# A causal convolution ahead of two matmul layers: units cut into overlapping blocks, five on TensorE and four off it

## The chip, the cores and the metric

The kernel runs on one core of a Trainium2 chip. A core has five engines that this text calls TensorE (PE in the profile, its weight loads PEld), VectorE (DVE), ScalarE (ACT), GpSimd (POOL) and SyncE (SP), which here issues nearly all transfers. The metric is the device time of one execution in microseconds (us); lower is better. Three runs of the kernel before gave 710.38, 710.92 and 711.0, a median of 710.92.

## The reference

`x` is 8 sequences of 4096 tokens with 192 channels in float32. There are 8 heads of 24 neighbouring channels; each has 7 taps, the softmax of a row of `weight`. The convolution looks back over 7 tokens, and every sequence begins with zeros:

```python
w = softmax(weight)                                   # 8 heads x 7 taps
x_pad = concatenate([zeros((B, 6, D)), x], axis=1)
out[b, s, h, g] = sum(w[h, k] * x_pad[b, s + k, h, g] for k in range(7))
```

The result, 32768 tokens by 192 channels, goes through two layers with a gate between them:

```python
h = x @ w_in            # 192 -> 2048
g = h * np.cos(h)
out = g @ w_out         # 2048 -> 192
```

## The kernel before, in words

**Tiles and units.** A tile `t` is 512 tokens, and there are 64. A unit `u` is 1024 tokens, two tiles: the even tile of the unit and the odd one. Four units make a sequence. Convolution, casts, loads and transposes go by units and are done some units ahead; the two layers go by tiles.

**The two layers.** `mm1(t, j)` makes 256 of the 2048 hidden columns of a tile, for j = 0 to 7; the text calls these eight h0 to h7. It takes three channel groups of 64, and each of them on the upper and the lower 64 rows of the array at once, so one h is six matmuls of 64 rows by 512 tokens (L475). The result fills one of three `h` buffers in PSUM, of two banks each. `gcu` puts the cosine on ScalarE (L483) and the product with h on VectorE (L487); the product frees the buffer. `mm2_step` (L525) adds pairs of such matmuls of 192 columns into the output banks `o_ps`, 64 steps a tile, while the next tile's h are made. Half-way through a tile's steps the two row halves change banks; a `Turn` (L176) makes TensorE's first matmul after the change wait for an empty instruction on the SP queue, which itself waits for the matmuls before the change. A tile's output is copied from PSUM by ScalarE and VectorE (`evac`, L544) and stored from SP (L547).

**The convolution before, from unit 4 on.** A unit has eight blocks of 128 tokens. Six of them (`NPE = UB - 2`) are convolved on TensorE: token rows times a band matrix per head, which holds the taps on its diagonals (`conv_mm`, L222). One `conv_part` does four heads, and a tile has one of them: 8 matmuls of 64 rows by 144 columns, 4 and 4 around a `Turn`, into an `h` buffer. ScalarE copies it out (`conv_out`, L237, two copies of 288 elements), GpSimd writes every 64 channels twice (`double_unit`, L290) so that both row halves get them, and one transposing transfer on SP (`turn_unit`, L303, 18 squares of 128 by 128) puts channels on partitions in `cT`.

The other two blocks are cast, transposed as they are (`turn_raw`, L321, with the edges 6 squares) and convolved with channels on partitions: ScalarE multiplies with three of the taps (`taps_act`, L327), GpSimd with four and adds (`conv_raw`, L336 to L342), and two transfers carry each result to the other row half (`spread_raw`, L349).

A block convolved by itself lacks the six tokens before it, so the first six tokens of every block are wrong. `load_edges` (L77) loads 16 tokens around each block's start, and `mend_edges` (L365 to L371) makes the six tokens again on GpSimd. Units 1 to 3 have smaller variants of this; unit 0 is done apart, at the start.

**What sets the order.** There is no scheduler: each engine runs its instructions in the order in which the code records them, and two strings of marks give this order for every tile. In the first, hj is an h, mN are N steps of the second layer, q the half-way change, c1 and c2 the halves of a `conv_part`, and K, T, L, X, Y, D, R, U, O cast, raw transpose, load, transpose, mend, double, raw convolution, spread and store. In the second, sj is cosine and product, aj.. a tap, e.. a conv copy, P and Q the two evacuations. P and the taps are ScalarE's, Q is VectorE's:

```python
PE_ORDER = "m11 h0 m4 h1 U m6 h2 m7 q Y R K h3 m7 h4 m7 c1 m4 c2 X T L m5 h5 m9 p h6 D O h7 m4"
ACT_ORDER = "s0 a00 s1 s2 a12 s3 s4 ec1 ec2 Q s5 P s6 s7 a27"
```

K, R and X are done in the even tile of a unit, and D, L, Y, T, U and the three taps in the odd one.

Of the kernel before, what the change touches and what calls it, by code (L numbers as in the profile page):

```python
# [16 lines left out]
def kernel(  # L17
# [8 lines left out]
    nc = tc.nc  # L26
# [18 lines left out]
    FIRST_RAW = 2 * 2  # L45
    NPE = UB - 2
    W = 128 - (K - 1)
    PA = 3

# [7 lines left out]
    raw_pool = ctx.enter_context(tc.tile_pool(name="raw", bufs=2))  # L57
# [77 lines left out]
    xb0 = xbf_pool.tile([128, UB + 1, D], BF16, name="x_bf")  # L135
# [17 lines left out]
    wn = consts.tile([128, HQ, K], BF16)  # L153

# [30 lines left out]
    bf = {}  # L185

    def cast_unit(u, n0=0, n1=UB + 1, copy=nc.gpsimd.tensor_copy):
        if n0 == 0:
            bf[u] = xb0 if u == 0 else xbf_pool.tile([128, UB + 1, D], BF16, name="x_bf")
        if u >= FIRST_RAW:  # L190
            raw[u] = raw_pool.tile([128, 2, NC, 2, 64], BF16, name="raw")

            def part(out, m0, m1):
                copy(out=out, in_=x_tiles[u][:, m0:m1, :].rearrange("p n (h r k) -> p (n h) k r", k=NC, r=R))  # L194


            for t in range(2):
                copy(out=raw[u][:, 0, :, t, :].rearrange("p k (h r) -> p h k r", r=R),  # L198
                     in_=x_tiles[u][:, NPE + t, :].rearrange("p (h r k) -> p h k r", k=NC, r=R))
            for t in range(2):  # L200
                copy(out=raw[u][:, 1, :, t, :].rearrange("p k (h r) -> p h k r", r=R),
                     in_=x_tiles[u][:, UB, :].rearrange("p (h r k) -> p h k r", k=NC, r=R))
            if u % UPS == 0:
                nc.gpsimd.memset(raw[u][0:8, 1], 0.0)
            part(bf[u][:, 0:NPE, :].rearrange("p n (h k r) -> p (n h) k r", k=NC, r=R), 0, NPE)
            bf.pop(u - 2, None)
            return
# [4 lines left out]
        if u and u % UPS == 0:  # L212
            nc.gpsimd.memset(bf[u][0:8, UB, :], 0.0)
        bf.pop(u - 2, None)
# [4 lines left out]
    def conv_mm(u, c, ps, i, rows, n0, n1, prev=0, **flags):  # L219

        h = 4 * c + i
        return nc.tensor.matmul(  # L222
            out=ps[i // 2][:, 0 : (n1 - n0) * 2 * G].rearrange("p (n k i r) -> p i n k r", n=n1 - n0, k=NC, i=2)[:, i % 2],
            lhsT=band[rows, h, 128 if prev else 0 : 256 if prev else 128],
            rhs=bf[u][rows, n0:n1, h * G : (h + 1) * G].rearrange("p n (k r) -> p n k r", k=NC),
            skip_group_check=True, **flags)

    def conv_out(u, c, ps, n0, m0, m1, copy, double=False, banks=(0, 1)):

        for b in banks:  # L230
            w0 = (2 * c + b) * 2 * R
            o = ct_tiles[u][:, m0:m1, :, :, w0 : w0 + 2 * R].rearrange("p n k t w -> p (n k) t w")
            i = ps[b][:, (m0 - n0) * 2 * G : (m1 - n0) * 2 * G].rearrange("p (m t w) -> p m t w", t=1, w=2 * R)
            if double:
                copy(o, i.to_broadcast([128, (m1 - m0) * NC, 2, 2 * R]))
            else:
                copy(o[:, :, 0, :], i[:, :, 0, :])  # L237
# [8 lines left out]
    def conv_part(u, c, banks, whole=False):  # L246
# [3 lines left out]
        nb = NPE if u >= FIRST_RAW else UB + (u == 1)  # L250
        sides = [slice(0, 64), slice(64, 128)]

        def mm(i, rows, **flags):
            return conv_mm(u, c, ps, i, sides[rows], 0, nb, **{"start": False, "stop": False, **flags})

        if whole:
            for i in range(4):
                conv_mm(u, c, ps, i, slice(0, 128), 0, nb, start=i % 2 == 0, stop=i % 2 == 1)
            if u == 2 and c == 0:
                spread_taps(ps[1][:, UB * 2 * G : UB * 2 * G + K])  # L260
            yield
        else:
            mm(0, 0, start=True)
            mm(2, 1, start=True)
            turn = Turn()
            turn.mark(mm(1, 0), mm(3, 1))
            yield
            turn.wait(mm(2, 0), mm(0, 1))
            mm(3, 0, stop=True)
            mm(1, 1, stop=True)  # L270
# [3 lines left out]
        for b in range(2):  # L274
            conv_out(u, c, ps, 0, 0, nb, nc.scalar.copy, banks=(b,))
            if b and u == 2 and c == 0:
                nc.scalar.copy(tap, ps[1][:, UB * 2 * G : UB * 2 * G + K])
            if b:
                have.add(("conv", u, c))
            yield  # L280
# [3 lines left out]
    def double_unit(u):  # L284
# [4 lines left out]
        nb = NPE if u >= FIRST_RAW else UB + (u == 1)  # L289
        nc.gpsimd.tensor_copy(out=ct[:, 0:nb, :, 1, :], in_=ct[:, 0:nb, :, 0, :])  # L290
        for t in range(2) if 1 < u < FIRST_RAW else ():
            nc.gpsimd.tensor_copy(out=ct[:, UB, :, t, :].rearrange("p k (h r) -> p k h r", r=R),
                                  in_=bf[u][:, UB, :].rearrange("p (h k r) -> p k h r", k=NC, r=R))

    def turn_unit(u, n0=0, n1=UB + 1):
        assert ("double", u) in have
        have.update((("turn", u), ("whole", u, 1)) if u == 0 else (("turn", u),))
        ct = ct_tiles.pop(u)
        if u >= FIRST_RAW:
            n1 = NPE  # L300
        if u not in cT:
            cT[u] = cT_pool.tile([128, UB + 1, NC, 128], BF16, name="cT")
        nc.sync.dma_start_transpose(out=cT[u][:, n0:n1].rearrange("p n c k -> p (n c) k"),  # L303
# [13 lines left out]
    raw, rT, pa = {}, {}, {}  # L317

    def turn_raw(u):
        rT[u] = rT_pool.tile([128, 2, NC, 128], BF16, name="rT")  # L320
        nc.sync.dma_start_transpose(out=rT[u].rearrange("p n c k -> p (n c) k"),  # L321
                                    in_=raw.pop(u).rearrange("p n c t k -> p (n c t k)"))

    def taps_act(u, j):
        if j == 0:
            pa[u] = pa_pool.tile([128, PA, NC, W], FP32, name="pa")
        nc.scalar.mul(pa[u][:, j], rT[u][:, 0, :, j : j + W], tap[:, j : j + 1])  # L327

    raw_prod = consts.tile([128, K - PA, NC, W], FP32)

    def conv_raw(u):

        cT[u] = cT_pool.tile([128, UB + 1, NC, 128], BF16, name="cT")
        a, p = pa.pop(u), raw_prod
        for j in range(PA, K):
            nc.gpsimd.tensor_scalar(out=p[:, j - PA], in0=rT[u][:, 0, :, j : j + W], scalar1=tap[:, j : j + 1], scalar2=None,  # L336
                                    op0=ALU.mult)
        nc.gpsimd.tensor_tensor(out=p[:, 0:PA], in0=p[:, 0:PA], in1=a, op=ALU.add)  # L338
        nc.gpsimd.tensor_tensor(out=p[:, 0:2], in0=p[:, 0:2], in1=p[:, 2:4], op=ALU.add)  # L339
        for t in range(2):  # L340
            rows = slice(64 * t, 64 * t + 64)
            nc.gpsimd.tensor_tensor(out=cT[u][rows, NPE + t, :, K - 1 : 128], in0=p[rows, 0], in1=p[rows, 1], op=ALU.add)  # L342

    def spread_raw(u):

        have.add(("raw", u))
        for t in range(2):
            of, to = slice(64 * t, 64 * t + 64), slice(64 - 64 * t, 128 - 64 * t)
            nc.sync.dma_start(out=cT[u][to, NPE + t, :, K - 1 : 128], in_=cT[u][of, NPE + t, :, K - 1 : 128])  # L349

    edge_prod = consts.tile([128, NC * UB, K - 1, K], FP32)

    def mend_edges(u):
# [3 lines left out]
        if u == 1:  # L357
            nc.gpsimd.tensor_copy(out=cT[u][:, 0:UB, :, 0 : K - 1],
                                  in_=cT[u][:, UB].rearrange("p c (n t) -> p n c t", t=16)[:, :, :, 8 : 8 + K - 1])
            return  # L360
        edges = rT.pop(u)[:, 1] if u >= FIRST_RAW else cT[u][:, UB]
        edges = edges.rearrange("p c (n t) -> p (c n) t", t=16)
        window = edges[:, :, 2 : 2 + K]
        window = bass.AP(window.tensor, window.offset, [*window.ap[:2], [1, K - 1], [1, K]])
        nc.gpsimd.tensor_tensor(out=edge_prod, in0=window,  # L365
                                in1=tap.rearrange("p (a b k) -> p a b k", a=1, b=1).to_broadcast([128, NC * UB, K - 1, K]),
                                op=ALU.mult)
        nc.gpsimd.tensor_tensor(out=edge_prod[:, :, :, 0:3], in0=edge_prod[:, :, :, 0:3], in1=edge_prod[:, :, :, 3:6], op=ALU.add)  # L368
        for j in (1, 2):
            nc.gpsimd.tensor_tensor(out=edge_prod[:, :, :, 0], in0=edge_prod[:, :, :, 0], in1=edge_prod[:, :, :, j], op=ALU.add)  # L370
        nc.gpsimd.tensor_tensor(out=cT[u][:, 0:UB, :, 0 : K - 1].rearrange("p n c t -> p c n t"),  # L371
# [322 lines left out]
```

## Time and profile before

| what | value |
|---|---|
| median of 3 runs | 710.92 us |
| the profiled execution, and its span | 710.74 us, 709.0 us |
| TensorE busy | 702.8 us, 99% |
| VectorE busy | 640.2 us, 90% |
| ScalarE busy | 621.0 us, 88% |
| GpSimd busy | 598.6 us, 84% |
| granted TensorE clock | 1.00 over the span |
| transfers' queue q1 | 50.3% of 16 engines' span |

Busy is the union of an engine's instructions; overlapping ones count once. A matmul's recorded end is modelled, so what TensorE really spends is read from start to start: a pair of matmuls on the two row halves starts some 216 ns after the last pair at 512 columns. Issuing a transfer isn't counted as busy, but it holds the queue that issues it for the time that its line shows. In a timeline's line the columns are start and length in us, engine, line of the code, operation, output<-input, shapes, and count; the bracket gives the idle time before it and who ended it.

The page's costliest groups of GpSimd, by line, mean length of one: L336 products 1209 ns (366 elements), L338 sums 2518 (1098), L339 sums 1738 (732), L342 sums 829 (366 on half the partitions), L365 edge products 2237 (1008), L368 1013 and L370 556 edge sums, L290 doubling 1144 (1152), L194 casts 1758 (1152). In two units, 299 to 342 us, these and the smaller ones keep GpSimd busy 40.4 of 43 us.

### The profile page before, as it was taken

What the parts mean: (1) busy time and instruction counts of PE and PEld (TensorE: products, weight loads), DVE (VectorE), ACT (ScalarE), POOL (GpSimd) and SP (SyncE); (2) the same over time, 40 slices, a digit from 0 to 9 for tenths busy, and PEclk for the clock granted to TensorE, in tenths of its full rate; (3) what the DMA queues carried; (4) which work ended last, traced back from release to release, by engine and by line L of the source; (5) the groups of instructions that cost most, each with busy time, mean ns of one, the idle gap of its engine ahead of it and who ended that gap; (6) DMA issues with size and microseconds to landing.
All of it is one profiled execution on the core that took longest, in us unless ns stands there. A gap on an engine that the chain in (4) does not pass through costs nothing.

```text
span 709.0 us, 27153 instructions
## 1 busy us (share of the span) xinstructions
PE 702.8 (99%) x11836; PEld 532.8 (75%) x11838; DVE 640.2 (90%) x598; ACT 621.0 (88%) x803; POOL 598.6 (84%) x588
## 2 busy tenths in 40 slices
PE   8999999999999999999999999999999999999997
PEld 4677777777777777777777777777777777777776
DVE  6889998999999999999999999999999999999996
ACT  7888989898989898998889898989898989988875
POOL 6554999999999999999999999999999999997900
PEclk9999999999999999999999999999999999999999
DMA  8974546446446455364465364564553553643311
GB/s 210 241 153 103 117 115 144 83 129 148 103 128 139 83 134 145 97 138 85 126 145 120 112 147 83 126 147 107 124 131 90 136 134 103 142 93 67 85 46 46
DMA packets 185510, 85.17 MB, mean 120 GB/s; under 512 B 113456, under 2 KB 185008, under 8 KB 185392
## 3 DMA queue, kind: packets, MB, share of 16 engines
q1 hardware_dynamic: 184680, 82.47, 50.3%
q8 instruction: 92, 1.51, 0.9%
q0 software_dynamic: 416, 0.79, 0.7%
q14 instruction: 26, 0.21, 0.1%
q10 hardware_dynamic: 296, 0.20, 0.1%
HBM read 31.36 MB, written 25.17 MB: 80 GB/s over the span
## 4 chain that ended last, share of the span: by engine, by line
PE 96%; DMA 1%; DVE 1%; POOL 0%; SPq 0%; ACT 0%; issue 0%; POOLq 0%
PE o_ps L525 47%; PE h L475 47%; PE h L222 2%; DMA wo_f<-in_moe_w_out_dram 1%; PE h L525 0%; SPq L105 0%; DVE band L393 0%; POOL wo L101 0%; POOL mask L140 0%; DVE ct L416 0%; PE o_ps L410 0%; ACT mask L145 0%; DVE diag L382 0%; DVE prod L379 0%; DVE o_sb L554 0%
## 5 line engine op out<-in xcount | busy, mean ns | idle before, releaser
L487 DVE TENSOR_TENSOR g<-h,cs 128x1024 bf16<-128x1024 f32 (+1 forms) x513 | 602.7, 1216 | 25.3 <-ACT cs L483 22.5
L483 ACT ACTIVATE cs<-h 128x1024 bf16<-128x1024 f32 (+1 forms) x513 | 509.4, 1023 | 69.2 <-PE h L475 54.9
L525 PEld LDWEIGHTS <-g 64*128 64x128 bf16 x8192 | 366.1, 94 | 92.0 <-issue 0.7
L525 PE MATMUL o_ps<-wo,g 64*128 64x192 bf16 x8128 | 430.4, 243 | 0.2 <-POOL wo L101 0.2
L475 PE MATMUL h<-cT,w 64*128 64x512 bf16 (+1 forms) x3078 | 411.7, 376 | 0.7 <-DVE g L487 0.4
L475 PEld LDWEIGHTS <-w 64*128 64x128 bf16 x3078 | 160.1, 94 | 71.1 <-issue 1.8
L336 POOL TENSOR_SCALAR raw_prod<-rT,tap 128x366 f32<-128x366 bf16 x112 | 133.6, 1209 | 0.0
L338 POOL TENSOR_TENSOR raw_prod<-raw_prod,pa 128x1098 f32<-128x1098 f32 x28 | 70.5, 2518 | 0.0
L544 DVE COPY o_sb<-o_ps 128x384 f32<-128x384 f32 x62 | 34.6, 557 | 34.1 <-PE o_ps L525 33.9
L365 POOL TENSOR_TENSOR edge_prod<-rT,tap 128x1008 f32<-128x1008 bf16 x28 | 62.6, 2237 | 0.2
L290 POOL COPY ct<-ct 128x1152 bf16<-128x1152 bf16 (+2 forms) x31 | 36.6, 1181 | 28.8 <-ACT ct L237 27.5
L237 ACT CAST ct<-h 128x288 bf16<-128x288 f32 (+2 forms) x124 | 44.8, 412 | 8.3 <-PE h L222 5.0
L339 POOL TENSOR_TENSOR raw_prod<-raw_prod 128x732 f32<-128x732 f32 x28 | 48.7, 1738 | 2.2
L327 ACT ACTIVATE pa<-rT,tap 128x366 f32<-128x366 bf16 x84 | 50.5, 601 | 0.0
L342 POOL TENSOR_TENSOR cT<-raw_prod 64x366 bf16<-64x366 f32 x56 | 46.4, 829 | 4.3
L194 POOL CAST x_bf<-x_f 128x1152 bf16<-128x1152 f32 x28 | 49.2, 1758 | 0.0
L222 PE MATMUL h<-x_bf,band 64*128 64x144 bf16 (+3 forms) x480 | 37.5, 224 | 0.0
L370 POOL TENSOR_TENSOR edge_prod<-edge_prod 128x144 f32<-128x144 f32 x60 | 33.4, 556 | 4.7
L368 POOL TENSOR_TENSOR edge_prod<-edge_prod 128x432 f32<-128x432 f32 x30 | 30.4, 1013 | 2.3
L544 ACT COPY o_sb<-o_ps 128x384 f32<-128x384 f32 x64 | 30.2, 473 | 0.1
L198 POOL CAST raw<-x_f 128x192 bf16<-128x192 f32 x56 | 23.4, 446 | 1.7
L222 PEld LDWEIGHTS <-band 64*128 64x128 bf16 (+1 forms) x480 | 22.7, 94 | 1.4 <-issue 1.1
(70 smaller groups left out, 109.3 us busy)
## 6 DMA issues: line engine op xcount, KB each, us to landing
out_dram<-o_sb SPq DMA_DIRECT2D x63, 384.0 KB, 3.0
x_f<-in_x_dram SPq DMA_DIRECT2D x30, 768.0 KB, 7.3
x_f<-in_x_dram SPq DMA_DIRECT2D x31, 96.0 KB
cT<-cT SPq DMA_DIRECT2D x56, 45.8 KB, 3.0
x_f<-in_x_dram SPq DMA_DIRECT2D x4, 384.0 KB, 5.7
wo_f<-in_moe_w_out_dram SPq DMA_DIRECT2D x4, 384.0 KB, 7.0
w<-in_moe_w_in_dram POOLq DMA_DIRECT2D x2, 384.0 KB, 6.2
cT<-ct SPq DMA_TRANSPOSE x32, 4.9
```

Source lines behind the costliest of these rows:

```text
L194: copy(out=out, in_=x_tiles[u][:, m0:m1, :].rearrange("p n (h r k) -> p (n h) k r", k=NC, r=R))
L222: return nc.tensor.matmul(out=ps[i // 2][:, 0 : (n1 - n0) * 2 * G].rearrange("p (n k i r) -> p i n k r", n=n1 - n0, k=NC, i=2)[:, i % 2], ...
L327: nc.scalar.mul(pa[u][:, j], rT[u][:, 0, :, j : j + W], tap[:, j : j + 1])
L336: nc.gpsimd.tensor_scalar(out=p[:, j - PA], in0=rT[u][:, 0, :, j : j + W], scalar1=tap[:, j : j + 1], scalar2=None, op0=ALU.mult)
L338: nc.gpsimd.tensor_tensor(out=p[:, 0:PA], in0=p[:, 0:PA], in1=a, op=ALU.add)
L339: nc.gpsimd.tensor_tensor(out=p[:, 0:2], in0=p[:, 0:2], in1=p[:, 2:4], op=ALU.add)
L365: nc.gpsimd.tensor_tensor(out=edge_prod, in0=window, in1=tap.rearrange("p (a b k) -> p a b k", a=1, b=1).to_broadcast([128, NC * UB, K - 1 ...
L475: nc.tensor.matmul(out=h[:, i, n0 * 128 : n1 * 128], lhsT=w[rows, k, j, :], rhs=c[rows, m0 + n0 : m0 + n1, k, :], start=(k == 0), stop=(k ...
L483: nc.scalar.activation(out=cs[:, :, part], in_=h[:, :, part], func=AF.Sin, bias=math.pi / 2.0, scale=1.0)
L487: nc.vector.tensor_tensor(out=g_tiles[t][:, 2 * j : 2 * j + 2, part], in0=h[:, :, part], in1=cs[:, :, part], op=ALU.mult)
L525: ms.append(nc.tensor.matmul(out=o_ps[tt, b, si], lhsT=g_tiles[tt][rows, f, s * 128 : (s + 1) * 128], rhs=wo[rows, f // 2, f % 2, :], star ...
L544: (copy or copies[b])(o_sb[t][:, 2 * b : 2 * b + 2, :].rearrange("p s d -> p (s d)"), o_ps.pop((t, b)))
```

## The change

**Blocks that overlap.** From unit 4 on a unit has nine blocks of 128 tokens that overlap (`load_unit`): five that each give 112 new tokens (`NPB, OP = 5, 112`), 560 together, and four that each give 116 (`NRB`, `OR`), 464 together. A block contains the tokens before its new ones, so there are no edges: `load_edges` and `mend_edges` are gone from unit 4 on, and units 1 to 3 have their edges from the band matrix, and only copied.

**On TensorE.** `conv_unit` takes the five blocks for all eight heads at once, once a unit, in the odd tile: 16 matmuls of 64 rows by 120 columns (15 pieces of 8 elements), 8 and 8 around one `Turn`. The weights are the last 112 columns of the band. Two copies of 480 elements go into `ct_bufs`, whose squares are 64 channels wide with an empty one at each group's ends. `turn_unit` then transposes without doubling: for each of three channel groups once from the first square and once from the second, so that the row halves hold the same tokens 112 columns apart. That makes six transfers of three squares of 112 by 128, in place of one of 18. `mm1` reads the two row halves at places that differ by `OP`.

**Off TensorE.** The four other blocks are cast into the same buffer `xk`, transposed (6 squares), and convolved with channels on partitions: three taps on ScalarE as six instructions of 348 elements, four taps on GpSimd as one instruction of 2784, then three sums of 2088, 1392 and 696 elements. `spread_raw` has four transfers for two.

**Order.** The two tiles of a unit now have their own strings. `R+1` means the raw convolution of unit u + 1, and `a211` tap 2, half 1, after h1.

```diff
-    NPE = UB - 2
-    W = 128 - (K - 1)
+    NPB, OP = 5, 112
+    NRB = 4
+    OR = (U - NPB * OP) // NRB
+    WN = NC * NRB // 2
     PA = 3
+    HALF = WN // 2
+    CW = U + OP
...
     def load_unit(u, n0=0, n1=UB, queue=nc.sync):
+        if u >= FIRST_RAW:
+            x_tiles[u] = xin.tile([128, UB + 1, D], FP32, name="x_f")
+            raw = NPB * OP + OR - 128
+            for n0, n1, t0, step in ((NPB, NPB + 2, raw, 2 * OR), (NPB + 2, UB + 1, raw + OR, 2 * OR), (0, NPB, OP - 128, OP)):
+                rows = xf[u * U + t0 : u * U + t0 + 128, :]
+                rows = bass.AP(rows.tensor, rows.offset, [[D, 128], [step * D, n1 - n0], [1, D]])
+                queue.dma_start(out=x_tiles[u][:, n0:n1, :], in_=rows)
+            return
...
     def cast_unit(u, n0=0, n1=UB + 1, copy=nc.gpsimd.tensor_copy):
+        if u >= FIRST_RAW:
+            xk[u] = xk_pool.tile([128, NC * (UB + 1), 64], BF16, name="xk")
+            for n0, n1 in ((NPB, UB + 1), (0, NPB)):
+                copy(out=xk[u][:, NC * n0 : NC * n1].rearrange("p (k n) m -> p k n m", k=NC),
+                     in_=x_tiles[u][:, n0:n1].rearrange("p n (m k) -> p k n m", k=NC))
...
+    def conv_unit(u, banks):
+        ps = banks()
+        sides = [slice(0, 64), slice(64, 128)]
+        def mm(h, side):
+            first, last = h % 4 == 0 and h // 4 == side, h % 4 == 3 and h // 4 != side
+            return nc.tensor.matmul(
+                out=ps[h // 4][0:OP, 0 : NPB * 4 * G].rearrange("p (m i r) -> p i m r", m=NC * NPB, i=4)[:, h % 4],
+                lhsT=band[sides[side], h, 128 - OP : 128], rhs=xk[u][sides[side], 0 : NC * NPB, R * h : R * (h + 1)],
+                start=first, stop=last, skip_group_check=True)
+        for h in range(4):
+            ms = mm(h, 0), mm(h + 4, 1)
+        turn = Turn()
+        turn.mark(*ms)
+        yield
+        for h in range(4):
+            ms = mm(h + 4, 0), mm(h, 1)
+            if h == 0:
+                turn.wait(*ms)
+        yield
+        for b in range(2):
+            w0 = 4 * R * b
+            nc.scalar.copy(ct_bufs[u % 2][0:OP, 0 : NC * (NPB + 1)].rearrange("p (k n) m -> p k n m", k=NC)[:, :, 1:, w0 : w0 + 4 * R],
+                           ps[b][0:OP, 0 : NPB * 4 * G].rearrange("p (k n w) -> p k n w", k=NC, w=4 * R))
...
     def turn_unit(u, n0=0, n1=UB + 1):
+        if u >= FIRST_RAW:
+            cT[u] = cT_pool.tile([128, NC * (UB + 1) * 128], BF16, name="cT")
+            for k in range(NC):
+                to = cT[u][:, k * CW : k * CW + (NPB + 1) * OP].rearrange("p (n s t) -> p s n t", s=2, t=OP)
+                for s in range(2):
+                    m = (NPB + 1) * k + s
+                    nc.sync.dma_start_transpose(out=to[:, s], in_=ct_bufs[u % 2][0:OP, m : m + NPB + 1].rearrange("p s m -> p (s m)"))
...
-    def taps_act(u, j):
+    def taps(u, j, half, mul):
+        part = slice(HALF * half, HALF * (half + 1))
+        mul(pa[u][:, j, part], tap_window(u, j)[:, part], tap[:, j : j + 1])
...
     def conv_raw(u):
+        nc.gpsimd.tensor_tensor(out=p, in0=tap_window(u, PA, K),
+                                in1=tap[:, PA:K].rearrange("p (j a b) -> p j a b", a=1, b=1).to_broadcast([128, K - PA, WN, OR]),
+                                op=ALU.mult)
...
     def spread_raw(u):
+        for to, t0 in ((0, NPB * OP + OP), (1, NPB * OP)):
+            rows = slice(64 * to, 64 * to + 64)
+            d = c[rows, :, t0 : t0 + NRB * OR].rearrange("p k (v t) -> p k v t", v=2)
+            for v in range(2):
+                nc.sync.dma_start(out=d[:, :, v], in_=r[64 * v : 64 * v + 64])
...
     def mm1(t, j, n0=0, n1=NB):
+                if t >= TPU * FIRST_RAW:
+                    t0 = k * CW + (t % TPU) * T + n0 * 128 + (0 if i else OP)
+                    rhs = c[rows, t0 : t0 + (n1 - n0) * 128]
...
-    PE_ORDER = "m11 h0 m4 h1 U m6 h2 m7 q Y R K h3 m7 h4 m7 c1 m4 c2 X T L m5 h5 m9 p h6 D O h7 m4"
-    ACT_ORDER = "s0 a00 s1 s2 a12 s3 s4 ec1 ec2 Q s5 P s6 s7 a27"
+    PE_ORDER = ['m12 h0 m4 h1 m5 R+1 h2 K+3 m7 q h3 m6 h4 m17 h5 U+0 X+1 m9 p h6 h7 O m4', 'm11 h0 m4 h1 m6 h2 m7 q h3 m5 h4 T+3 m7 c1 m8 c2 L+4 m3 h5 m9 O h6 p h7 m4']
+    ACT_ORDER = ['s0 s1 a211 s2 s3 s4 a014 a114 Q s5 P s6 s7 a007', 's0 s1 s2 a102 s3 a203 s4 Q ec2 ec1 s5 P s6 s7']
```

More of the change, by code (lines that the diff above doesn't have):

```diff
@@ L132 @@
     keep_warm(9)
-    xb0 = xbf_pool.tile([128, UB + 1, D], BF16, name="x_bf")
+    xb0 = consts.tile([128, UB + 1, D], BF16, name="x_bf0")
     E = 32 + K - 1
@@ L153 @@
     wn = consts.tile([128, HQ, K], BF16)
+    ct_bufs = [consts.tile([128, NC * (NPB + 1) + 1, 64], BF16, name="ct_buf%d" % i) for i in range(2)]
     wmax = consts.tile([128, HQ, 1], FP32)
@@ L182, in wait @@
                 tc.add_manual_dep(m.ins, self.nop.ins.name, sync_dep, reason="row halves on one bank")
-    bf = {}
+    bf, xk = {}, {}
     def cast_unit(u, n0=0, n1=UB + 1, copy=nc.gpsimd.tensor_copy):
+        if u >= FIRST_RAW:
[3 more added lines that the diff above has]
+                     in_=x_tiles[u][:, n0:n1].rearrange("p n (m k) -> p k n m", k=NC))
+            if u % UPS == 0:
+                nc.gpsimd.memset(xk[u][0 : 128 - OP, 0 : NC * NPB : NPB], 0.0)
+            return
         if n0 == 0:
             bf[u] = xb0 if u == 0 else xbf_pool.tile([128, UB + 1, D], BF16, name="x_bf")
[L190 to L207, printed above, removed]
         o = 1 if u == 0 else 0
@@ L249, in conv_part @@
         ps = banks()
[L250 to L270, printed above, removed]
+        nb = UB + 1
+        for i in range(4):
+            conv_mm(u, c, ps, i, slice(0, 128), 0, nb, start=i % 2 == 0, stop=i % 2 == 1)
+        if u == 1 and c == 0:
+            spread_taps(ps[1][:, nb * 2 * G : nb * 2 * G + K])
+        yield
         yield
@@ L288, in double_unit @@
         ct = ct_tiles[u]
[L289 to L293, printed above, removed]
-    def turn_unit(u, n0=0, n1=UB + 1):
+        nc.gpsimd.tensor_copy(out=ct[:, :, :, 1, :], in_=ct[:, :, :, 0, :])
+    def turn_unit(u, n0=0, n1=UB + 1):
+        if u >= FIRST_RAW:
+            assert {("conv", u, 0), ("conv", u, 1)} <= have
+            have.update((("whole", u, 0), ("whole", u, 1)))
+            cT[u] = cT_pool.tile([128, NC * (UB + 1) * 128], BF16, name="cT")
[4 more added lines that the diff above has]
+                    nc.sync.dma_start_transpose(out=to[:, s], in_=ct_bufs[u % 2][0:OP, m : m + NPB + 1].rearrange("p s m -> p (s m)"))
+            cT.pop(u - 2, None)
+            return
         assert ("double", u) in have
@@ L315, in spread_taps @@
                              start=i == 0, stop=i == 1, skip_group_check=True)
[L317 removed]
+    rT, pa, ro = {}, {}, {}
     def turn_raw(u):
[L320 to L327 removed]
@@ L331, in conv_raw @@
+    raw_prod = consts.tile([128, K - PA, WN, OR], FP32)
     def conv_raw(u):
-        cT[u] = cT_pool.tile([128, UB + 1, NC, 128], BF16, name="cT")
         a, p = pa.pop(u), raw_prod
[L335 to L339, printed above, removed]
@@ L340, in conv_raw @@
-        for t in range(2):
-            rows = slice(64 * t, 64 * t + 64)
-            nc.gpsimd.tensor_tensor(out=cT[u][rows, NPE + t, :, K - 1 : 128], in0=p[rows, 0], in1=p[rows, 1], op=ALU.add)
+        nc.gpsimd.tensor_tensor(out=p, in0=tap_window(u, PA, K),
+                                in1=tap[:, PA:K].rearrange("p (j a b) -> p j a b", a=1, b=1).to_broadcast([128, K - PA, WN, OR]),
+                                op=ALU.mult)
+        add = nc.gpsimd.tensor_tensor
+        n, done = K - PA, 0
@@ L344, in spread_raw @@
+        while done < PA:
+            m = min(n, PA - done)
+            add(out=p[:, 0:m], in0=p[:, 0:m], in1=a[:, done : done + m], op=ALU.add)
+            done += m
+        while n > 2:
+            m = n // 2
+            add(out=p[:, 0:m], in0=p[:, 0:m], in1=p[:, n - m : n], op=ALU.add)
+            n -= m
+        ro[u] = ro_pool.tile([128, WN, OR], BF16, name="ro")
+        add(out=ro[u], in0=p[:, 0], in1=p[:, 1], op=ALU.add)
     def spread_raw(u):
         have.add(("raw", u))
-        for t in range(2):
-            of, to = slice(64 * t, 64 * t + 64), slice(64 - 64 * t, 128 - 64 * t)
-            nc.sync.dma_start(out=cT[u][to, NPE + t, :, K - 1 : 128], in_=cT[u][of, NPE + t, :, K - 1 : 128])
@@ L396 @@
     nc.gpsimd.memset(pick, 0.0)
+    for b in range(2):
+        nc.gpsimd.memset(ct_bufs[b][0:OP, 0 : NC * (NPB + 1) + 1 : NPB + 1], 0.0)
     for i in range(2):
@@ L433, in turn_first @@
                                  start=True, stop=True, skip_group_check=True)
-            copies[n](out=cT[0][:, 2 * half + n].rearrange("p c k -> p (c k)"), in_=ps[:, 0 : NC * 128])
+            m = NC * (2 * half + n)
+            copies[n](out=cT[0][:, m * 128 : (m + NC) * 128], in_=ps[:, 0 : NC * 128])
     def conv_rest():
@@ L580 @@
         for i, part in enumerate("dc"):
-            conv[part, v] = conv_part(v, i, ring_banks, v < 3)
+            conv[part, v] = conv_part(v, i, ring_banks)
     step, made, stored, done = 0, -1, 0, set()
@@ L608, in flush @@
                         evac(made, int(k != "P"), nc.scalar.copy if k == "A" else None)
-                elif k[0] == "a":
-                    if second and u + 2 in rT:
-                        taps_act(u + 2, int(k[1]))
+                elif k[0] in "ab":
+                    if u + 2 in rT:
+                        taps(u + 2, int(k[1]), int(k[2]), nc.scalar.mul if k[0] == "a" else nc.vector.tensor_scalar_mul)
                 elif k[0] == "e":
@@ L624, in of_unit @@
                 load_unit(v)
-                load_edges(v)
+                if v < FIRST_RAW:
+                    load_edges(v)
             else:
```

94 lines of the change are left out of this document (43 added, 51 removed), and 5 rows, old and new, of tables (ACT_FIRST, PE_FIRST).

## The prediction

> **What bounds the kernel now.** The page comes first: its busy shares, then the chain of work that ended last.
>
> ```profile
> PE 702.8 (99%) x11836; PEld 532.8 (75%) x11838; DVE 640.2 (90%) x598; ACT 621.0 (88%) x803; POOL 598.6 (84%) x588
> PE 96%; DMA 1%; DVE 1%; POOL 0%; SPq 0%; ACT 0%; issue 0%; POOLq 0%
> ```
>
> TensorE is the chain, but four engines stand at 84% or more, so cover is thin. The chain in order of time gives the length of a tile: the start of one h x12 entry (h6 and h7) to the next.
>
> ```profile
> 333.81 1.29 PE h L475 x12
> ...
> 344.52 1.30 PE h L475 x12
> ...
> 355.36 1.29 PE h L475 x12
> ...
> 667.45 1.29 PE h L475 x12
> ...
> 677.91 1.30 PE h L475 x12
> ```
>
> Tiles alternate between 10.71 and 10.84 us, 21.55 for a unit of two; the last tiles, without convolution, take 10.46. Two bare tiles are 20.92, so a unit's convolution costs 0.63. TensorE's timeline shows of what; the first three lines are of an odd tile, the last two of an even one.
>
> ```profile
> 353.15 0.30 PE L222 MATMUL h<-x_bf,band 64*128 64x144 bf16 x4
> 353.28 0.59 PE L525 MATMUL o_ps<-wo,g 64*128 64x192 bf16 x10
> 353.80 0.82 PE L475 MATMUL h<-cT,w 64*128 64x512 bf16 x6
> ...
> 364.09 0.59 PE L525 MATMUL o_ps<-wo,g 64*128 64x192 bf16 x10
> 364.50 0.83 PE L475 MATMUL h<-cT,w 64*128 64x512 bf16 x6
> ```
>
> Four convolution matmuls (two pairs on the row halves) take 0.125 us to the next group's start (0.13 here, 0.12 at other places, as 363.51 to 363.63), 62.5 ns a pair; eight pairs make 0.50. The rest, 0.13, is a stall of the odd tile: L525 to L475 is 0.52 there and 0.41 in the even one. ScalarE's timeline of the odd tile says why.
>
> ```profile
> 347.74 1.02 ACT L483 ACTIVATE cs<-h 128x1024 bf16<-128x1024 f32 x1 [0.59 <-PE h L475]
> 348.66 0.59 ACT L327 ACTIVATE pa<-rT,tap 128x366 f32<-128x366 bf16 x1
> 349.15 1.93 ACT L483 ACTIVATE cs<-h 128x1024 bf16<-128x1024 f32 x2
> ```
>
> A tap stands between two cosines; all three of a unit's taps are in the odd tile, with two conv copies. So cosines and products (g) come late, and h5, which takes its h buffer from h3, waits for h3's product.
>
> **TensorE's part.** Sixteen matmuls of 144 columns become sixteen of 120. By L222 (62.5 ns at 144 columns), 82 ns a pair at 192 (L525) and 216 at 512 (L475), a pair takes 0.417 ns a column and 2.3 more: 52 ns at 120. Eight pairs: 0.42 for 0.50, a gain of 0.08 a unit. All of it is on the path. Inner runs of the moving operand shrink from 24 elements to 8; no row has that, the written side already has runs of 8 at full rate, and I take no cost.
>
> **The stall** goes if the new orders leave every buffer in time. From the timelines: a cosine starts 0.86 us after its h starts and holds ScalarE 0.91; a tap holds it 0.49 (348.66 to 349.15) at 366 elements, so a half tap of 348 about 0.48; g starts 1.06 after its cosine and not under 1.14 after the last g; its buffer is free 1.28 after it starts. A conv copy of 480 elements holds ScalarE about 0.5 (384 take 0.47 at L544). The new odd tile, starts in us from its h0:
> - h: 0, 0.98, 2.12, 3.35, 4.41, conv 5.64 and 6.51, h5 6.97, h6 8.36, h7 9.01.
> - cosines: 0.86, 1.84, 2.98, tap 3.89, 4.37, tap 5.28, 5.76, copies 6.94 and 7.42, 7.9, evacuation 8.81, 9.28, 10.19.
> - g: 1.92, 3.06, 4.20, 5.43, 6.82, evacuation 8.5, 8.97, 10.34, 11.48.
> - buffers, free then needed: h3 3.20/3.35, h4 4.34/4.41, conv 5.48/5.64, h5 6.71/6.97, h6 8.10/8.36, the next h0 10.25/10.97.
> The even tile, now with four half taps and no convolution, comes out alike: h3 3.20/3.27, h4 4.34/4.41, h5 5.57/6.46. No wait is left, but margins are 0.07 us: between 0 and the present 0.13 of stall can stay. I take 0.03, nearer the worked value. ScalarE's total grows: six half taps for three whole (2.9 for 1.5), two copies for four (1.0 for 1.3): 19.28 busy of a unit's 21.55 become about 20.4 of 21.35, still under.
>
> **GpSimd.** The doubling (1.14), the edge sums (2.24, 1.01, 1.11, 0.61) and small casts go. New a unit: casts of 768 and 960 elements, 1.23 + 1.49 (L210 has both sizes); products of 2,784 elements at the 2.22 ns an element of the edge products (2237/1008), 6.2; sums of 2,088, 1,392 and 696 at 2.3 (2518/1098), 9.6. Together 18.5 of 21.35 against 20.03 before. Were the products as slow as L336 (1209/366, 3.3 ns) it would be 21.5 and GpSimd the bound; they are nearest to L365, whose operands have the same form. The casts end about 7 us into a unit (products can start before the taps are there; the sums wait for the last tap, 16.2 into the unit before), and the raw transpose that waits for them is issued at 13.9, so the SP queue does not stand at it.
>
> **The SP queue** carries 16 transfers a unit for 8, and also the waits (L176) by which TensorE's second row half follows the first. In the profile before:
>
> ```profile
> 353.15 1.24 SPq L321 DMA_TRANSPOSE rT<-raw  x1
> ...
> 363.97 2.72 SPq L303 DMA_TRANSPOSE cT<-ct  x1
> 366.79 0.53 SPq L547 DMA_DIRECT2D out_dram<-o_sb  x1
> 367.43 1.32 SPq L349 DMA_DIRECT2D cT<-cT  x2
> ```
>
> Transposes of 6 and 18 blocks take 1.24 and 2.72: 0.12 a block on 0.5. Three blocks would be 0.86. Below nothing is excluded; a transfer issued for itself takes at least 0.38 (L547 in the odd tile), and the six-block row caps it: 0.38 to 1.24. After the even tile's wait (3.6 us) come four spreads (0.72 each with gaps), six transposes (0.94) and two stores (1.25): 9.8, done 3.1 into the odd tile, where the next wait is marked at 3.6 and h3 covers TensorE until 4.0. So nothing. Of the rest, three loads and one transpose lie behind the odd tile's waits, with 3 us to spare or more; spread data and cT are needed 4 us or more after they land (3.0 and 4.9 us by the page).
>
> **Start and end.** Units 1 to 3 take nine blocks through whole-array matmuls, +0.16 us in all; GpSimd has less to do there, two small memsets apart, which stand where it next waits 0.76 for wo. The last tiles are the same.
>
> **Sum.** -0.08 - 0.13 + 0.03 = -0.18 a unit, by 28 units -5.0, +0.2 at the start: -4.8. The profiled execution took 710.74 (span 709.0), 0.18 under the median of 710.92: 706.0. Differences under 0.2%, 1.4 us, can't be told from none.
>
> **Rivals.**
> *Weights in the way (slower).* The convolution's weight loads go from 128 columns to 112. Each bf16 load of the trace has 128, and two hide in a pair of 62.5 ns, so fewer columns should hide in 52. But L222's loads are recorded at 94 ns, and the one load of another kind (L131, 4x128 f32) at 283 to 332. If a 112-column load can't be overlapped with its own half's last one, a pair takes the load. Three of the four pairs of a group would show it: a unit is 20.92 + 6p + 0.10, and from p = 88 ns it is slower than 21.55. At 94 with both halves side by side 21.58, +1 us, 712; with the halves one after the other, 188, 22.15, +17, 728; at 616 (two of L131's) +89, 800, for which nothing speaks but that row. The Trainium skill, "TensorE: Matmul & The Clock Gate", section on the weight-path modes, has this rule: fast weight load is on only when the weights are 128 columns. Its LDWEIGHTS section gives columns over 1.2 ns, an estimate of 93 ns for 112, by which the sum would be 712; no run so far has such a load.
>
> *SP late.* If a short transpose takes over 1.0 us, SP reaches the odd tile's wait after 4.0 and TensorE stands there, six times the excess a unit: at 1.24 that is 1.3 us, 742. For it: transfers in a burst queue behind each other's landing (before, eight a unit never did). Against: 18 blocks are 18 blocks.
>
> *The stall stays.* Cosines and products as late as now: only 0.08 of gain, -2.2 + 0.2, 708.7. The 0.07 margins speak for it; that taps are spread over both tiles against.
>
> *GpSimd as the bound*, 21.5 a unit: 709.5 to 712.
>
> **Numbers.** Forecast, 703.5 to 708.5: 0.50. Stall stays, to 709.5: 0.10. Weights side by side, 709.5 to 714: 0.17. Weights in a row: 0.08. SP late: 0.12. GpSimd: 0.03. Faster: the first two but a little, 0.57; within 1.4 us of 710.74: half of the side-by-side case and bits, 0.10; slower 0.33. The range must keep the weights case and mild lateness of SP: 703.5 to 718, leaving out the long ends; the likeliest case's own is 703.5 to 708.5.
>
> **What would show it.** Right: tiles of about 10.4 and 11.0 (21.35 to 21.4 a unit), four conv matmuls 0.105 apart, L525 to the next L475 without 0.1 extra, TensorE's chain unbroken. Weights: conv matmuls further apart than 0.12 for four. SP: the wait's event after h3's end, and PE idle before the first L525 matmul that follows. Wrong throughout would be ScalarE over 21 us busy a unit or short transposes past 1 us.

## The result, and the profile after

The changed kernel takes 764.85 us (median of 4 runs, 759.45 to 767.69) where the kernel before takes 710.65 (710.36 to 711.0, 4 runs): a ratio of 1.0753 (its 95% interval is [1.0693, 1.0814], and so in brackets below), 7.5% slower. The forecast was 706.0 with a range to 718. Of the rivals it is the one called *SP late*. The profiled execution is the shortest of the four, 759.45 us, with a span of 757.7.

From the page of the changed kernel, first the busy times, then the chain that ended last:

```profile
PE 703.5 (93%) x11828; PEld 508.5 (67%) x11830; DVE 642.7 (85%) x598; ACT 647.1 (85%) x831; POOL 497.6 (66%) x214
PE 87%; ACT 6%; issue 3%; SPq 1%; DMA 1%; POOL 1%; DVE 0%; POOLq 0%
```

TensorE is as many microseconds busy as before (703.5 for 702.8), but of a span 48.7 us longer. No engine rose to the bound; TensorE stands idle. The chain's 6% of ScalarE come in through the issues of stores on SP, as at 346.96 us, but SP's timeline below has no pause there. The table of waits says behind what (who waits, for whom, us in total, times, longest):

```profile
PE o_ps L553 <- SPq L194: 47.9, 27, 2.8
```

L194 is the `Turn`: the empty instruction on SP that releases TensorE's first matmul after the change of row halves. In the kernel before this wait has no line of its own; now it costs 47.9 us in 27 places, one per unit. TensorE's timeline gives tile and place:

```profile
339.03 1.46 PE L504 MATMUL h<-cT,w 64*128 64x512 bf16 x12
347.39 0.59 PE L553 MATMUL o_ps<-wo,g 64*128 64x192 bf16 x10 [1.67 <-SPq L194]
351.76 1.46 PE L504 MATMUL h<-cT,w 64*128 64x512 bf16 x12
362.22 1.46 PE L504 MATMUL h<-cT,w 64*128 64x512 bf16 x12
```

The x12 lines are h6 and h7 of successive tiles, the first of an even one. From 339.03 to 351.76, with the odd tile's front half in it, are 12.73 us, where the forecast had about 11.0 by tiles counted from h0; from 351.76 to 362.22 are 10.46. The 1.67 us of idle are in the odd tile alone. Counted from h0, the even tile is always 10.38 long, the odd one 12.15 to 14.87, 12.98 in the mean. In the first units, in which no spreads are on the queue yet, the tiles are 10.38 and 10.96, which is the forecast.

SP's timeline shows what it did meanwhile (start and length in us):

```profile
334.71 2.59 SPq L386 DMA_DIRECT2D cT<-ro  x4
337.41 8.70 SPq L316 DMA_TRANSPOSE cT<-ct_buf  x6
346.23 1.05 SPq L575 DMA_DIRECT2D out_dram<-o_sb  x2
```

From the first spread to the end of the stores is 12.57 us without a break: it ends at 347.28, and TensorE goes on at 347.39. The forecast had 9.8 for the same work, with 0.9 us to spare (done at 3.1, TensorE covered till 4.0). It is 2.8 over, so 1.9 beyond the spare; 1.67 of idle and 0.18 more, which nearly every stalled tile takes beside its idle time (25 of 27), are 1.85. All of the excess is in the six transposes: 8.70 and a gap of 0.1 where 5.64 was reckoned (six of 0.94). One source line says what a single one takes; the three figures are shortest, median and longest, in ns:

```profile
L316 SPq DMA_TRANSPOSE cT<-ct_buf x168: 1177/1251/2850, 81.2 to 719.9; - x168
```

Three squares hold SP for 1.25 us, as long as the six squares of the raw transpose did before (1212/1245/2194). The forecast had 0.86.

### The profile page after: what moved, and what is told of

Same layout as the page of the kernel before. It is cut to its first block, busy times and chain, and to the rows that moved or that the text cites. A ratio compares the mean times of both kernels' runs of the same rounds, so it can differ in the third digit from the quotient of the medians.

```text
span 757.7 us, 27001 instructions
## 1 busy us (share of the span) xinstructions
PE 703.5 (93%) x11828; PEld 508.5 (67%) x11830; DVE 642.7 (85%) x598; ACT 647.1 (85%) x831; POOL 497.6 (66%) x214
## 4 chain that ended last, share of the span: by engine, by line
PE 87%; ACT 6%; issue 3%; SPq 1%; DMA 1%; POOL 1%; DVE 0%; POOLq 0%
PE o_ps L553 43%; PE h L504 41%; ACT cs L511 4%; ACT pa L354 2%; PE h L275 2%; SPq L575 1%; DMA x_f<-in_x_dram 1%; PE h L553 0%; PE h L227 0%; POOL x_bf L217 0%; DVE g L515 0%; POOL mask L157 0%; PE o_ps L134 0%; ACT mask L162 0%; DVE diag L403 0%
## 5 line engine op out<-in xcount | busy, mean ns | idle before, releaser
L553 PE MATMUL o_ps<-wo,g 64*128 64x192 bf16 x8128 | 420.7, 243 | 47.9 <-SPq L194 47.9
L553 PEld LDWEIGHTS <-g 64*128 64x128 bf16 x8192 | 350.7, 94 | 159.0 <-SPq L194 61.2
L368 POOL TENSOR_TENSOR raw_prod<-raw_prod,pa 128x2088 f32<-128x2088 f32 x28 | 128.9, 4605 | 169.3 <-ACT pa L354 169.2
L361 POOL TENSOR_TENSOR raw_prod<-rT,tap 128x2784 f32<-128x2784 bf16 x28 | 135.2, 4830 | 0.2
L354 ACT ACTIVATE pa<-rT,tap 128x348 f32<-128x348 bf16 x168 | 94.5, 579 | 0.0
L372 POOL TENSOR_TENSOR raw_prod<-raw_prod 128x1392 f32<-128x1392 f32 x28 | 87.8, 3137 | 2.2
L209 POOL CAST xk<-x_f 128x768 bf16<-128x768 f32 (+1 forms) x56 | 75.0, 1368 | 0.0
L375 POOL TENSOR_TENSOR ro<-raw_prod 128x696 bf16<-128x696 f32 x28 | 46.4, 1659 | 2.2
L292 ACT CAST ct_buf<-h 112x480 bf16<-112x480 f32 x56 | 28.5, 561 | 18.2 <-PE h L275 17.9
L275 PE MATMUL h<-xk,band 64*112 64x120 bf16 x448 | 21.5, 216 | 0.0
L275 PEld LDWEIGHTS <-band 64*112 64x112 bf16 x448 | 18.4, 130 | 0.0
```

What stands on the lines that cost most here:

```text
L209: copy(out=xk[u][:, NC * n0 : NC * n1].rearrange("p (k n) m -> p k n m", k=NC), in_=x_tiles[u][:, n0:n1].rearrange("p n (m k) -> p k n m", ...
L275: return nc.tensor.matmul(out=ps[h // 4][0:OP, 0 : NPB * 4 * G].rearrange("p (m i r) -> p i m r", m=NC * NPB, i=4)[:, h % 4], lhsT=band[si ...
L354: mul(pa[u][:, j, part], tap_window(u, j)[:, part], tap[:, j : j + 1])
L361: nc.gpsimd.tensor_tensor(out=p, in0=tap_window(u, PA, K), in1=tap[:, PA:K].rearrange("p (j a b) -> p j a b", a=1, b=1).to_broadcast([128, ...
L368: add(out=p[:, 0:m], in0=p[:, 0:m], in1=a[:, done : done + m], op=ALU.add)
L372: add(out=p[:, 0:m], in0=p[:, 0:m], in1=p[:, n - m : n], op=ALU.add)
```

## The experiments

Two theories were on the table. **S**: the burst of short transposes on SP holds up the odd tile's wait. **D**: the transfers slow one another on their way, wherever they are issued, and that holds TensorE. Besides, the burst could be a bystander while something else in the new order (late cosines, late convolution, weight loads) makes TensorE stop. And, inside S, there are three ways to read the price of 1.25 us: a square of 112 rows is dear (H1), every transpose has a floor (H2), or the gaps in what is written cost (H3). All changes below are to the changed kernel, if not said otherwise.

**1. The same transfers at another place.** Only the mark of the four spreads moves, from the even tile, just ahead of the burst, to the end of the odd tile before it, behind the loads.

```diff
-    PE_ORDER = ['m12 h0 ... m17 h5 U+0 X+1 m9 p h6 h7 O m4', '... c2 L+4 m3 h5 m9 O h6 p h7 m4']
+    PE_ORDER = ['m12 h0 ... m17 h5 X+1 m9 p h6 h7 O m4', '... c2 L+4 U+1 m3 h5 m9 O h6 p h7 m4']
```

> The changed kernel with the four spread transfers moved from the even tile (between the even tile's half-way wait and the odd tile's) to the odd tile, behind the loads, one tile earlier for the unit that needs them. Theory S, the SP queue is late: after the even tile's wait at 3.5 us only six transposes (1.30 each with gaps) and two stores (1.07) are left, 8.9 us, done 2.0 into the odd tile, before its wait is marked at 3.6; the stall is gone, a unit takes 21.35 and the kernel 705 to 707 us. Theory D, the transfers slow one another on their way and that holds TensorE: their number a unit is the same, so 750 or more.

Measured: 705.75 us (705.18 to 706.83), a ratio of 0.9935 [0.992, 0.9949] to the kernel before. One mark is worth 59.1 us. TensorE's busy share, and from its chain the h6 and h7 of three tiles:

```profile
PE 696.9 (99%) x11830; PEld 511.2 (73%) x11830; DVE 642.8 (91%) x598; ACT 644.5 (91%) x831; POOL 498.0 (71%) x214
```

```profile
342.67 1.29 PE h L504 x12
353.55 1.29 PE h L504 x12
364.00 1.29 PE h L504 x12
```

10.88 and 10.45, 21.33 for a unit, where the forecast had 21.35. SP's timeline has the burst as long as ever:

```profile
359.59 8.42 SPq L316 DMA_TRANSPOSE cT<-ct_buf  x6
368.12 1.05 SPq L575 DMA_DIRECT2D out_dram<-o_sb  x2
```

The transfers take what they took (8.50 us a burst in the mean of 27 units, 8.53 of 28 in the changed kernel). What changed is that 2.6 to 3.7 us of spreads no longer stand between the even tile's wait and the odd tile's. The orders of the other engines are as in the changed kernel, and the number of transfers is the same, by which D forecast 750 or more. So S holds, and the total forecast for a kernel without this stall, 706.0, was right to 0.25 us.

**2. A smaller dose.** Of the same stretch of SP, only the even tile's store goes (the odd tile's `O` then issues both).

```diff
-... m17 h5 U+0 X+1 m9 p h6 h7 O m4
+... m17 h5 U+0 X+1 m9 p h6 h7 m4
```

> The changed kernel with both stores of a unit issued in the odd tile, none in the even one: a dose. Theory S: 1.07 us less stand on the SP queue between the even tile's wait and the odd tile's; the odd tile's stall of about 1.9 us a unit shrinks by that, by 28 units 30 us: 730 to 738. Theory D: no difference, 758 to 768.

Measured: 725.5 us (724.17 to 725.93), ratio 1.0204 [1.0187, 1.0221], a little under what was expected. The wait is what is left of it:

```profile
PE o_ps L553 <- SPq L194: 15.9, 23, 1.5
```

About 1.1 us less on the queue takes 1.2 us off an odd tile (11.75 for 12.98 in the mean). Where the queue is late, the odd tile pays for it nearly one for one; the bystanders on other engines were left as they are, so they don't explain the difference.

**3. What a transpose costs, by form.** Six extra transposes a unit from the cast buffer into scratch that nobody reads, behind the odd tile's loads: 112 or 128 rows, three or six squares, squares side by side or with gaps. Its total time (832.47 us, one run) says nothing, as the queue is overfull.

```diff
+    kinds = [(rows, n, step) for n in (3, 6) for step in (1, 2) for rows in (112, 128) if n == 3 or step == 1]
+            nc.sync.dma_start_transpose(out=scratch[i].rearrange("p (n s t) -> p s n t", s=step, t=rows)[:, 0],
+                                        in_=xk[u][0:rows, 0 : 2 * n].rearrange("p s m -> p (s m)"))
```

> The changed kernel with six more transposes a unit into scratch, behind the loads of the odd tile, of different forms and in turned order in every other unit: 3 squares of 112 and of 128 rows, each written contiguously and with gaps, 6 squares of 112 and of 128 rows. It prices the issue. H1, a square of 112 rows costs as two: 3 squares of 112 take 1.25 us with and without gaps, 3 of 128 0.86, 6 of 128 1.24, 6 of 112 2.0. H2, no transpose is under 1.2 us: all four of 3 squares take 1.2, 6 of 128 1.24. H3, the gaps in what is written cost: 0.86 without gaps, 1.25 with. The time of this kernel itself says nothing.

```profile
L395 SPq DMA_TRANSPOSE scratch<-xk x156: 1174/1258/3098, 74.9 to 736.1; - x156
```

Medians in ns, in the two orders in which they were issued: three squares of 112 rows 1251 and 1183; of 128 rows 1257 and 1254; 112 with gaps 1252 and 1251; 128 with gaps 1255 and 1256; six squares of 112 rows 1483 and 1282; of 128 rows 1272 and 1291. Rows and gaps make next to no difference, and six squares cost nearly what three do; H1 had 2.0 us for six squares of 112 rows, H3 0.86 for three without gaps. It is H2: in 156 transposes none took under 1.17 us.

**4. The split in the kernel before.** The unit's transpose of 18 whole squares is issued as six of three. Nothing else of the change is in.

```diff
-        nc.sync.dma_start_transpose(out=cT[u][:, n0:n1]..., in_=ct[:, n0:n1]...)
+        for m0, m1 in [(m, m + 1) for m in range(n0, n1)] if u >= FIRST_RAW else [(n0, n1)]:
+            nc.sync.dma_start_transpose(out=cT[u][:, m0:m1]..., in_=ct[:, m0:m1]...)
```

> The kernel before, with each unit's transpose of 18 whole squares issued as six of 3. If 3 whole squares take 0.86 us (H1 or H3): on SP 6.2 + 6 x 0.92 + 0.6 + 1.4 = 13.7 us after the even tile's start, before the odd tile's wait is marked at 14.3: no change, 709 to 712. If they take 1.2 (H2): 16.0, against 14.7 when TensorE needs it, 1.3 us a unit, 744 to 750; theory D would have it slower too, but with no wait on SP's instruction.

Measured: 780.9 us (778.8 to 781.78), ratio 1.0986 [1.0969, 1.1004]. The sign and the mechanism are as expected, the size is not: 31 to 37 us more. SP, and TensorE in the tile after:

```profile
350.26 8.43 SPq L304 DMA_TRANSPOSE cT<-ct  x6
```

```profile
360.86 0.75 PE L526 MATMUL o_ps<-wo,g 64*128 64x192 bf16 x14 [1.98 <-SPq L176]
```

The same number of squares, of the same form, in the same order of work: 2.72 us in one transfer before, 8.43 in six. That alone makes TensorE stand 60.1 us in 27 waits. Of the excess over the expectation some 7 us is a slower clock behind the stalls (last section), and some 22 us the burst itself: 8.59 us in the mean of 28 units, where the expectation's sum left 7.8. The rest was not taken apart. The page's chain of this run goes by GpSimd for 59%, but GpSimd isn't what holds the burst: in 26 of 27 units the burst starts within 0.02 us of the second half of the even tile's convolution (here both at 350.26), the queue then works without a pause to 360.75, and TensorE goes on at 360.86.

**5. The changed kernel with two transposes.** The three groups' squares get a common distance (ten squares, the second half empty up to the group's end), so that one transfer of 13 squares replaces three of three. The spreads write over the places of the empty squares. They stay in the even tile, where the change put them. The buffers and the places that the spreads write to are fitted to this.

```diff
-    CW = U + OP
+    CW = 10 * OP
+    NSQ = 5 * (NC - 1) + 3
-            for k in range(NC): ... for s in range(2): ...
+            to = cT[u][:, 0 : NSQ * 2 * OP].rearrange("p (n s t) -> p s n t", s=2, t=OP)
+            for s in range(2):
+                nc.sync.dma_start_transpose(out=to[:, s], in_=ct_bufs[u % 2][0:OP, s : s + 2 * NSQ].rearrange("p s m -> p (s m)"))
...
```

> The changed kernel with a unit's six transposes of 3 squares made two of 13 (nine squares that are used and four empty ones, whose place the spread transfers write over afterwards); the spreads stay in the even tile. Theory S with a price for each transfer: two of 13 squares at 0.5 + 13 x 0.12 = 2.1 us in place of six at 1.25; SP has 2.7 + 0.4 + 4.3 + 1.2 = 8.6 us between the even tile's wait and the odd tile's, done 1.7 into the odd tile; no stall, 705 to 707 us. A theory by which the squares or the bytes moved cost (39 squares' worth of work for 18) would have it at 764 or more.

Measured: 706.39 us (706.35 to 706.51), ratio 0.9943 [0.993, 0.9957]. SP's timeline:

```profile
338.56 2.96 SPq L385 DMA_DIRECT2D cT<-ro  x4
341.64 3.34 SPq L315 DMA_TRANSPOSE cT<-ct_buf  x2
345.10 1.48 SPq L575 DMA_DIRECT2D out_dram<-o_sb  x2
```

More squares (26 for 18) in fewer transfers: 3.34 us for 8.70. Tiles are 10.38 and 10.96, and no wait on SP is left. So overlapping blocks are not what costs, and the spreads may stay where the change put them: the loss comes from what SP has to issue between two waits, and the six transposes are the larger part of it (8.70 of 12.57 us). A further kernel with both repairs, two transposes and the spreads in the odd tile, gives nothing more:

> Two long transposes and the spreads in the odd tile together. Theory S: SP then has 5.5 us where 10 are free, nothing is left to gain by either alone: 704.5 to 706, as the first experiment. If SP's load still cost something there (fetches that lengthen an issue), up to 0.7 us less than the first.

706.4 us (706.3 to 706.47), ratio 0.9943 [0.9931, 0.9956], a little above what was expected. With either repair alone SP is in time.

**6. The weight loads.** On top of experiment 1, the convolution's weights go from 112 columns to 128 (the 16 rows more that this computes are used by nobody).

```diff
-                out=ps[h // 4][0:OP, ...], lhsT=band[sides[side], h, 128 - OP : 128], ...
+                out=ps[h // 4][:, ...], lhsT=band[sides[side], h, 128 - OP : 256 - OP], ...
```

> The first experiment's kernel (spreads in the odd tile), the convolution's weights with 128 columns in place of 112 (the 16 rows more of the result aren't used). If 112 columns had a price on the path, this is faster than 705.75; if the loads hide, as the 52 ns a pair of the changed kernel suggest, it is the same within 0.2%, with loads recorded at 94 ns in place of 130.

Measured: 705.41 us (705.2 to 705.72), ratio 0.993 [0.9916, 0.9943]: within 0.05% of experiment 1. The rows of the loads, first with 128 columns, then with 112 (of experiment 1):

```profile
L275 PEld LDWEIGHTS <-band x448: 94/94/94, 72.4 to 649.9; 64*128 64x128 bf16 x150
```

```profile
L275 PEld LDWEIGHTS <-band x448: 127/127/127, 73.0 to 651.1; 64*112 64x112 bf16 x150
```

A load of fewer columns is recorded 33 ns longer, and the path does not show it.

**7. Only the taps moved, in the kernel before.** One of the three taps goes from the odd tile to the even one, which has no taps; the other two stay where they were.

```diff
-    ACT_ORDER = "s0 a00 s1 s2 a12 s3 s4 ec1 ec2 Q s5 P s6 s7 a27"
+    ACT_ORDER = "s0 s1 s2 a02 a12 s3 s4 ec1 ec2 Q s5 P s6 s7 a27"
-                    if second and u + 2 in rT:
+                    if second == (k[1] != "0") and u + 2 in rT:
```

> The kernel before with one change: tap 0 is made in the even tile after its third cosine, taps 1 and 2 stay in the odd one. If the odd tile's 0.13 us is ScalarE's order, as the working had it, it goes: 28 x 0.13 = 3.6 us, 706.5 to 707.5. If the stall has another cause, 710.5 stays.

Measured: 706.88 us (706.79 to 707.36), ratio 0.9951 [0.9938, 0.9965]. Its chain:

```profile
428.56 1.29 PE h L475 x12
439.26 1.29 PE h L475 x12
449.97 1.30 PE h L475 x12
```

All tiles are 10.71 now; the 0.13 us of the odd tile are gone, 28 of them make 3.6 us, and the gain is 3.55. So the stall was ScalarE's order, as the forecast read it from the trace, and three quarters of what experiment 1 gains on the kernel before (4.75 us) can be had without overlapping blocks.

## Why the prediction was wrong, and where it was right

**The step that failed** is the price of one short transpose: "Transposes of 6 and 18 blocks take 1.24 and 2.72: 0.12 a block on 0.5. Three blocks would be 0.86." A straight line through two rows was carried on below both. Under six squares there is a floor of 1.25 us (experiment 3); and 13 squares take 1.44 as a unit's first transpose and 1.89 as its second, in the median (experiment 5), where the line gives 2.06, so it isn't straight between them either. The margin was in the text: over 1.0 us SP is late, "at 1.24 that is 1.3 us, 742" (by the text's own rule, six times 0.24, it is 1.4 and some 746). The nearest row, of which the text itself said that it caps the price, was the right one to take. The argument against the rival, "18 blocks are 18 blocks", counted squares; below six squares the queue's price is for the transfer.

**Between 742 and 759 to 768.** A unit loses 2.0 us, not 1.3. The forecast took 0.08 us of gap for each transposing transfer on top of the price; in the traces a burst of six is 8.53 us in the mean of 28 units (7.92 to 9.79), 1.42 each. Six medians of 1.25 and five gaps of 0.04 are 7.7; the other 0.8 is single issues that run long, about one in each burst (last section). The other terms of that stretch, spreads and stores, were priced slightly too high (4.13 for 3.64 here). The 0.18 us that a stalled tile takes beside its idle time makes 4.9 in all: with the 47.9 that is 52.8, and with 1.7 us at a slower clock (last section) 54.5, where the spans of the changed kernel and of experiment 1 differ by 52.7 (in experiment 1's profiled execution two odd tiles are 0.3 and 0.7 us longer than the rest). The other three executions, 764 to 768 us, lost more to the clock (last section).

**Right, by the rest of the working.** *Convolution pairs at 52 ns*: eight matmuls of 120 columns take 0.21 us to the next group's start, in the timeline of the changed kernel:

```profile
349.04 0.38 PE L275 MATMUL h<-xk,band 64*112 64x120 bf16 x8
349.25 0.82 PE L553 MATMUL o_ps<-wo,g 64*128 64x192 bf16 x16
```

*The stall of 0.13 goes, 0.03 is kept*: units are 21.34 where SP is in time, for 21.35 forecast, and experiment 7 shows the cause by itself. The working of the buffers with margins of 0.07 us held. *ScalarE* was put at 20.4 of 21.35; in experiment 1 it is busy 40.45 of 43 us, 20.1 for a unit of 21.34.

*Weights*: the rival was excluded rightly, but on weak grounds. The words "fewer columns should hide" took the load for shorter, but it is recorded at 127 ns for a pair of 52, longer than the 94 of a full one. What is recorded is therefore not what holds up the path; how the loads overlap was not taken apart. The Trainium skill, "TensorE: Matmul & The Clock Gate", in the section on weight-path modes, has fast loading only at 128 columns; the 94 and 127 ns of experiment 6 agree with that. The estimate of 93 ns from the Trainium skill's section on LDWEIGHTS does not agree with the 127 recorded. Nor does the time follow the rival's formula, which would have put a unit from p = 88 ns above the kernel before: p stayed 52.

*GpSimd*: 18.5 forecast; 34.23 of 43 us in experiment 1, 17.0 a unit, measured. The one instruction for four taps was the term too high:

```profile
L361 POOL TENSOR_TENSOR raw_prod<-rT,tap 128x2784 f32<-128x2784 bf16 x28 | 135.2, 4830 | 0.2
```

4.83 us for the 6.2 taken from the edge products, whose rate was the nearest row but an instruction a third as long.

**The chances.** The rival that came true had 0.12 and a price of its own from a row of the same trace; against it stood only a line through two points. With a spare of 0.15 us a transfer (0.9 over six) it came true from 1.01 on; of the bounds, 0.38 to 1.24, a quarter lies above that, and the nearest row with it, so it should have had more than a quarter.

## What to carry to other kernels

On a queue that issues in order and also carries the waits of another engine, count the transfers and not only the bytes: cutting one transpose into six made its 2.7 us on the queue 8.4 while the data stayed the same. List what stands between each two waits, with the time by which the second must be through; a burst that is harmless elsewhere is paid for there one for one. And price an operation smaller than any in the trace at the nearest row, until a run shows that it gets cheaper.

## What the runs showed of the hardware

**A floor of some 1.2 us for a transposing transfer on SP**, up to six squares, whatever rows or gaps; plain transfers in the same timelines take 0.4 to 0.7 in the median. The first of a burst takes 1.21 even after 3.7 us in which SP issued nothing (experiment 1), so a full queue isn't the reason. It is a floor and not a fixed price: the raw transpose of six squares, at 1.25 us in the kernel before and 1.23 in experiment 5, takes 1.88 in the changed kernel, where it stands right behind the late burst and its stores. No run took this apart.

**A stall can cost its length again in clock.** In the changed kernel, after the wait of 2.09 us that ends at 371.0, TensorE goes on at full speed for 1 us and then runs at half speed for 3.4. Busy time of each engine in three stretches, and behind them the granted clock, DMA share and GB/s:

```profile
371.00:372.00 1.00, 1.00 (x16) 0.71 (x18) 0.39 (x1) 0.00 (x0) 1.00 (x1) 1.00 1.03 323
372.00:375.60 3.60, 3.60 (x57) 3.40 (x53) 1.22 (x1) 1.26 (x2) 3.52 (x2) 0.53 0.86 227
375.60:377.00 1.40, 1.40 (x28) 1.05 (x24) 0.00 (x0) 1.31 (x3) 1.40 (x1) 0.99 0.90 252
```

A clock of 0.53 over 3.6 us is half speed for 3.4 of them, and half of that, 1.7, is lost. In the profiled execution it happens after one of 27 waits, and in experiment 4 after four (those that end at 188.1, 237.1, 263.2 and 312.0 us, of 1.97 to 2.81), where the mean clock is 0.991: 0.9% of 777 us is 7.0. Longer waits, of 2.77 us in the changed kernel and 3.09 in experiment 4, left the clock alone, so length alone does not decide it. The Trainium skill, "TensorE: Matmul & The Clock Gate", section "What's actually happening", has a gate that halves the clock after at least one idle window of about 3.4 us and counts in windows that run freely; 3.4 us at half speed fits the window's length, but here waits of 2 us were enough. The clock also accounts for most of the 8 us over which the runs of the changed kernel spread: its mean over the execution of 759.45 us is 0.998, and 0.991 over each of the other three (764.07 to 767.69). Of 757.7 us, 0.007 are 5.3, where these are 4.6 to 8.2 us longer. Their traces were not kept, so the single windows can't be counted.

**Issues that run long.** Of 446 issues on SP in the changed kernel (after the first 70 us), 81 overlap a 16 KB transfer of the queue that the page calls q8 instruction; these are 0.43 us longer than the median of their line of code, in the mean, and the other 365 are as long as it (0.00). Of the issues over 0.3 us too long, all 44 overlap one. It is much the same in experiments 1, 2, 4 and 5 (0.36 to 0.48 us), and less in the kernel before (0.24, of 53). This is a correlation; no run took these transfers away or doubled them.
